# A fused retention and channel-mix kernel: the mu transfers go to SyncE's queue, more products of zeros ahead of the first transposes, and the pieces in a new written order

## The chip, the cores and the metric

The kernel runs on one core of one Trainium2 chip. The metric is the device time of one execution in microseconds (us). TensorE (PE) multiplies matrices, VectorE (DVE) and ScalarE (ACT) work on elements, GpSimd (POOL) and SyncE (SP) issue transfers here; ACT issues some transfers too.

## The reference, cut to what matters

```python
# attention: batch 4, 8 heads, 768 steps, head size 64
for t in range(S):
    state = gamma[None, :, None, None] * state + np.einsum('bhd,bhe->bhde', k[:, :, t], v[:, :, t])
    y[:, :, t] = scale * np.einsum('bhd,bhde->bhe', q[:, :, t], state)
x = y with the heads side by side                       # (4, 768, 512)

# channel mix: model size 512, inner size 1024
xk = mu_k * x + (1.0 - mu_k) * x_prev                   # x_prev: x one step earlier
xr = mu_r * x + (1.0 - mu_r) * x_prev
k = np.maximum(xk @ w_k, 0.0)
v = k * k @ w_v
r = 1.0 / (1.0 + np.exp(-(xr @ w_r)))
return r * v
```

## The kernel before, in words

**Tiling.** The sequence of each batch is cut into blocks of 256 steps: 4 x 3 = 12 blocks, numbered n = 0 to 11. For each block q and k are loaded, cast to f16 and transposed on PE (or, for q and k of blocks 9 to 11, by the transfer engines). Scores are formed within the block, masked on DVE and multiplied by the scaled v; a state of the earlier steps is carried from block to block. The result y is scaled into xT (`yout`, L570 and L577), the difference to the step before is formed (`differ`, L592), mixed with mu (`mixed`, L618), and goes through three products: keys with w_k (`keys`, L632 and L642), gate with w_r (`gate`, L672) and values with w_v (`values`, L684). ACT applies relu (L651), square (L659, L663) and sigmoid (L678), DVE multiplies gate and values (`result`, L690), and SP stores (`store`, L697).

**Order.** Nothing is scheduled automatically. The string `ORDER` (L28 to L79) lists all pieces. A loop at the end of the function reads it word by word and writes the instructions of each piece; each engine runs its own in that order and waits on semaphores for what it needs. A word is a code, the numbers of block and part, behind `~` the engine (v, a, p, s) and behind `@` the banks of the eight PSUM banks that it writes. So a change in the order of the words counts only as far as it changes the order on one engine or queue, and a change of bank changes which earlier reader a writer waits for.

**The codes in question.** `lq`, `lk`, `lv` load q, k, v (`load`, L239); for block 0 the first halves of q and k (heads 0 to 3, `0.0.2`) are loaded as f32 by SP into a staging place (`EARLY`, L245) and cast by ACT (`cq`, `ck`, L262); the second halves (`0.2.4`) come by POOL. `Tq` and `Tk` are transposes on PE (L303 to L314), `Eq` and `Ek` copy them from PSUM on ACT (L262). `S` are the scores (L372, L385, L393), `M` the mask on DVE (L417), `C` the new state (L458), `U` its addition, `gy` the powers of gamma (`gy.1~a` on ACT, L776). `Qa` and `Qb` are relu and square on ACT, `X` the mixing and `O` the result on DVE, `R`, `V` and `K` products on PE, `s` the sigmoid.

**Products of zeros.** `z.N` (`zeros`, L755) multiplies zeros into a bank that is free; nobody reads the result. N // 4 of them are f32 products (L758) and N % 4 are f16 products (L765), each with 512 columns.

**mu.** The word `mu` issues four transfers of 1 KB (`load_mu`, L739): two halves each of mu_k and mu_r into 8 rows of `mu8`. `mt` turns them on PE (L748), and `me` copies them on ACT (L751). The first written words are `gy.0 lq.0.0.2~s mu lk.0.0.2~s cq.0.0.2~a`. Ahead of the order, `constants` (L729) has ACT issue the transfers of two tables and run a small activation on a tile `warm`, and DVE clear some tiles.

Of the kernel before, what the change touches and what calls it, by code (L numbers as in the profile page):

```python
# [44 lines left out]
Tq.7@23 Eq.7~a V.1.1.0@1 V.1.1.1 G.4~a Qb.2.0 dx.3~v V.0.0.1 Tk.5@2 Ek.5~a D.4~v dx.4~v V.0.1.1
Qb.2.3 V.1.0.1 Tq.5@2 X.3.0.3 X.3.0.1 X.3.0.2 Eq.5~a X.3.0.0 K.3.1@3 Qa.3.1 K.3.3@4 O.1.1 O.0.0
S.5.0@01 O.1.0 O.0.1 lv.5~p lq.6~p M.5.0~v S.5.1@23 vs.5~v K.3.2@5 Qa.3.3 lk.6~p Qb.3.3 K.3.5@4
M.5.1~v X.2.1.0 Qa.3.2 X.2.1.2 Tq.6@67 Qa.3.5 Tk.6@01 Eq.6~a lv.6~p lv.7~p Ek.6~a C.5@5 U.5.0
X.3.1.0 Qb.3.1 K.3.0@4 Qa.3.0 lk.7~p K.3.7@6 S.6@23 Qb.3.2 M.6~v I.5@01 Y.5 vs.6~v V.2.1.0@7
R.2.1@2 lv.10~p Qb.2.2 Qa.3.7 K.3.4@6 st.0.0 vs.7~v Qb.3.7 s.2.1 st.0.1 V.2.1.1 Tk.7@45 Qb.3.5  # L50
Qa.3.4 X.3.1.3 X.3.1.1 Qb.3.0 C.6@23 st.1.0 J.5 Ek.7~a X.3.1.2 R.2.0@6 lv.8~p U.6.0~a D.5~v
U.6.1 U.6.2 U.6.3 V.2.0.0@4 s.2.0 K.3.6@6 dx.5~v Qa.3.6 lq.8~p lk.8~p st.1.1 R.4.1@5 I.6@01
O.2.1 st.2.1 X.5.0.1 s.4.1 G.6~a V.2.0.1 O.2.0 X.5.1.0 X.5.0.3 R.3.1@6 s.3.1 C.7@23 U.7.0 S.7@45
Y.6 M.7~v V.3.1.0@7 X.5.0.2 D.6~v R.4.0@6 lk.9~p Qb.3.4 vs.8~v V.3.0.0@4 R.3.0@5 X.5.1.2 s.4.0
Qb.3.6 V.4.1.0@6 V.3.0.1 V.3.1.1 X.5.1.3 V.4.1.1 U.7.1 U.7.2 X.5.1.1 I.7@01 U.7.3 Tk.8@23 O.3.1
s.3.0 O.3.0 R.5.1@7 Ek.8~a st.3.1 lv.9~p dx.6~v X.5.0.0 s.5.1 C.8@45 Tq.8@23 Y.7 K.5.0@7 O.4.1
# [6 lines left out]
Qb.6.6 V.5.1.1 K.6.2@4 Qa.6.2 X.8.0.1 Qb.6.2 K.6.5@3 tq.9~s Qa.6.5 R.6.1@4 s.6.1 tq.11~s st.5.0
K.6.0@6 O.5.1 U.9.2 U.9.3 G.9~v R.6.0@7 s.6.0 R.7.1@4 Qb.6.4 s.7.1 st.5.1 K.8.3@7 Qa.8.3 S.9@23
tk.11~s I.9@45 Qa.6.0 Qb.6.0 Qb.6.5 C.10@01 U.10.0 M.9~v R.7.0@7 s.7.0 U.10.1 U.10.2 U.10.3
K.8.2@6 K.8.1@2 Qa.8.1 vs.11~v Qb.8.1 V.6.0.0@7 Y.9 I.10@01 C.11@23 G.10~v V.6.0.1 Qa.8.2
V.7.1.0@6 D.9~v K.8.0@4 Qa.8.0 Qb.8.0 Qb.8.2 U.11.0 U.11.1 U.11.2 V.7.1.1 dx.9~v O.7.1 st.7.1
Qb.8.3 I.11@23 Y.10 D.10~v dx.10~v X.9.0.0 S.11@45 M.11~v X.9.0.2 V.7.0.0@6 V.7.0.1 V.6.1.0@0
V.6.1.1 V.8.0.0@1 V.8.0.1 X.9.0.1 V.8.1.0@4 V.8.1.1 st.4.0 X.9.0.3 K.9.0@5 O.7.0 K.9.4@6 X.9.1.1
Qa.9.0 Qa.9.4 Qb.9.4 X.9.1.0 O.6.0 st.6.0 Qb.9.0 X.9.1.3 X.8.1.2 Y.11 X.9.1.2 O.6.1 K.9.2@5  # L70
Qa.9.2 Qb.9.2 K.9.6@6 Qa.9.6 X.8.1.3 K.9.7@7 Qa.9.7 Qb.9.7 K.9.1@0 Qa.9.1 Qb.9.1 K.9.3@5 Qa.9.3
Qb.9.3 R.10.0@7 R.9.1@0 s.9.1 st.6.1 D.11~v R.9.0@5 s.9.0 st.7.0 X.8.1.1 K.9.5@6 V.10.1.0@5
Qa.9.5 Qb.9.5 Qb.9.6 V.10.0.0@6 X.8.1.0 dx.11~v R.8.1@0 s.8.1 V.9.1.0@2 R.8.0@0 X.11.0.2
X.11.1.3 X.11.0.0 X.11.0.3 X.11.0.1 K.11.1@3 s.8.0 K.11.3@0 Qa.11.3 O.8.0 st.8.0 s.10.0
# [8 lines left out]
def kernel(  # L83
# [328 lines left out]
    def masked(e, n, *part):  # L412
        src, dst = scored(n, *part)
        if part:
            seen.setdefault(n, []).append((part + (0, NJ))[:3])
# [1 line left out]
        nc.vector.tensor_tensor(  # L417
            out=dst, in0=dst if n in SPLITM else src,
            in1=mask[:, None, None, :].to_broadcast(list(dst.shape)), op=ALU.mult,
# [319 lines left out]
    def load_mu(e):  # L739
        for w, x in enumerate((moe_mu_k, moe_mu_r)):  # L740
            y = x.rearrange("(x r c) -> x r c", x=2, c=D)
            for hp in range(2):
                nc.scalar.dma_start(
                    out=mu8[w * NCO : (w + 1) * NCO, low(hp)], in_=y[:, 1:3] if hp else y[:, 0:4:3]
                )

# [108 lines left out]
```

## Time and profile before

| | us |
|---|---|
| median of 3 runs | 155.42 (155.16 to 155.71) |
| the profiled execution, whole | 155.54 |
| its span, first to last instruction | 153.7 |
| PE busy | 147.1 |
| DVE busy | 128.1 |
| ACT busy | 94.4 |
| POOL busy | 62.1 |

The profile is one execution. Times in it count from the first instruction of its span. A row of the timeline has the start, the length, the engine, the line of the kernel, the operation, what is written from what is read, the shape, how many instructions are merged into the row, and in brackets how long the engine had been idle and what ended that. The chain of waits goes back from the last instruction to whatever released each step. Matmuls are pipelined and their ends are modelled, so a filled PE is not always PE at its peak. A name such as SPq or ACTq is the queue of an engine from which transfers are issued; q0, q1 and q10 are the transfer queues that POOL, SP and ACT feed.

### The profile page before, as it was taken

To read this page: it belongs to the slowest core of one execution; us is meant where nothing else is said; L and a number is where in the kernel's file an instruction comes from. 1 tells how busy PE (TensorE), PEld (TensorE's weight loads), DVE (VectorE), ACT (ScalarE), POOL (GpSimd) and SP (SyncE) were. 2 spreads that over 40 slices of the span, in tenths; PEclk is the share of its full clock that TensorE was granted. 3 is DMA by queue.
4 is the path that set the end of the run, shared out by engine and by line. 5 is a ranking of instruction groups with operands and counts; after the bars stand their busy time and mean duration, and the time that the engine had idled before them with its cause. 6 is when DMAs were issued, how large, how long until landed. Compare 5 with 4: busy or idle time off the path is not lost.

```text
span 153.7 us, 4956 instructions
## 1 busy us (share of the span) xinstructions
PE 147.1 (96%) x2129; PEld 82.7 (54%) x2129; DVE 128.1 (83%) x204; ACT 94.4 (61%) x172; POOL 62.1 (40%) x77
## 2 busy tenths in 40 slices
...
GB/s 138 264 234 194 182 237 235 157 196 203 194 188 203 249 226 194 11 236 156 255 178 249 219 156 161 183 62 106 35 4 141 0 70 141 0 0 136 68 205 136
DMA packets 56525, 23.83 MB, mean 155 GB/s; under 512 B 48056, under 2 KB 52024, under 8 KB 56504
## 3 DMA queue, kind: packets, MB, share of 16 engines
...
q1 hardware_dynamic: 10848, 8.26, 21.9%
q10 hardware_dynamic: 456, 0.32, 0.8%
...
q14 instruction: 5, 0.04, 0.1%
...
## 4 chain that ended last, share of the span: by engine, by line
PE 70%; DVE 14%; DMA 6%; ACT 4%; issue 2%; ACTq 2%; DVEq 0%
PE ps L684 24%; PE ps L672 12%; PE ps L632 10%; PE ps L642 9%; DMA kT<-k 6%; DVE a L417 3%; DVE xk L618 3%; DVE dx L592 2%; DVE vs L277 2%; PE ps L504 2%; PE ps L765 2%; DVE xT L577 2%; PE ps L308 2%; PE ps L372 1%; PE ps L303 1%
## 5 line engine op out<-in xcount | busy, mean ns | idle before, releaser
L684 PE MATMUL ps<-wv,k2s 128*128 128x512 f16 x184 | 43.9, 380 | 0.2 <-ACT kr L651 0.2
L651 ACT ACTIVATE kr<-ps 128x512 f32<-128x512 f32 x48 | 27.8, 594 | 23.4 <-PE ps L632 14.9
L684 PEld LDWEIGHTS <-k2s 128*128 128x128 f16 x184 | 17.3, 98 | 19.1
L690 DVE SCALAR_TENSOR_TENSOR os<-ps,rs 128x512 f32<-128x512 f32 x23 | 15.1, 683 | 12.9 <-PE ps L684 6.5
L672 PE MATMUL ps<-wr,xr 128*128 128x512 f16 x96 | 24.0, 380 | 0.0
L642 PE MATMUL ps<-xk,wk 128*128 128x256 f16 x192 | 23.6, 273 | 0.1
L256 POOL DMA_DIRECT2D v<-in_v_dram x20 | 18.0, 917 | 13.8 <-DVE vs L277 10.9
L632 PE MATMUL ps<-xk,wk 128*128 128x512 f16 x96 | 22.8, 380 | 0.0
L417 DVE TENSOR_TENSOR a<-ps,c_sb 128x1024 f16<-128x1024 f32 (+1 forms) x20 | 21.8, 1109 | 0.8 <-PE ps L393 0.8
L678 ACT ACTIVATE rs<-ps 128x512 f32<-128x512 f32 x24 | 14.3, 594 | 11.4 <-PE ps L672 8.8
L642 PEld LDWEIGHTS <-wk 128*128 128x128 f16 x192 | 18.1, 98 | 4.4 <-DVE xk L618 0.5
L618 DVE SCALAR_TENSOR_TENSOR xr<-dx,mu,xT 128x256 f16<-128x256 f32 (+1 forms) x36 | 19.3, 564 | 0.0
L618 DVE SCALAR_TENSOR_TENSOR xk<-dx,mu,xT 128x256 f16<-128x256 f32 (+1 forms) x36 | 18.9, 567 | 0.3
L256 POOL DMA_DIRECT2D k<-in_k_dram x20 | 17.8, 916 | 2.6 <-DMA wv<-in_moe_w_v_dram 1.2
L277 DVE TENSOR_TENSOR vs<-v,csm_sb 128x1024 f16<-128x1024 f32 x12 | 14.5, 1214 | 2.7 <-DMA v<-in_v_dram 2.7
L659 ACT ACTIVATE k2s<-kr 128x512 f16<-128x512 f32 x24 | 14.7, 626 | 0.4
L592 DVE TENSOR_TENSOR dx<-xT 128x1024 f32<-128x1024 f32 x12 | 14.6, 1219 | 0.2
L663 ACT ACTIVATE k2s<-kr 128x512 f16<-128x512 f32 x24 | 14.5, 626 | 0.3
L632 PEld LDWEIGHTS <-wk 128*128 128x128 f16 x96 | 9.0, 98 | 10.5 <-issue 0.2
L672 PEld LDWEIGHTS <-xr 128*128 128x128 f16 x96 | 9.0, 98 | 10.0
L262 ACT COPY qT<-ps 128x1024 f16<-128x1024 f16 (+1 forms) x10 | 9.2, 925 | 7.5 <-PE ps L314 3.4
L262 ACT COPY kT<-ps 128x1024 f16<-128x1024 f16 (+1 forms) x10 | 9.3, 934 | 7.1 <-PE ps L303 3.4
...
## 6 DMA issues: line engine op xcount, KB each, us to landing
out_dram<-os SPq DMA_DIRECT2D x23, 256.0 KB, 3.9
v<-in_v_dram POOLq DMA_DIRECT2D x20, 256.0 KB, 6.3
k<-in_k_dram POOLq DMA_DIRECT2D x21, 128.0 KB, 7.1
q<-in_q_dram POOLq DMA_DIRECT2D x13, 128.0 KB, 7.4
q<-in_q_dram POOLq DMA_DIRECT2D x5, 256.0 KB, 8.1
...
wk<-in_moe_w_k_dram POOLq DMA_DIRECT2D x2, 256.0 KB, 9.6
```

Of the source, the lines that this page charges most:

```text
L256: e.dma_start(out=to[:, i, hs], in_=src[:, i])
L262: e.copy(out=out, in_=in_)
L277: e.tensor_tensor(out=VS(n), in0=V32(n).rearrange("p (h i d) -> p i h d", i=2, h=H), in1=gks[:, int(half(n) or wide(n)), :, :, None].to_br ...
L417: nc.vector.tensor_tensor(out=dst, in0=dst if n in SPLITM else src, in1=mask[:, None, None, :].to_broadcast(list(dst.shape)), op=ALU.mult,)
L592: e.tensor_tensor(out=DX(k)[:, :, m * TM + t0 : m * TM + t1], in0=x[:, :, c + t0 : c + t1], in1=x[:, :, c - 1 + t0 : c - 1 + t1], op=ALU.s ...
L618: nc.vector.scalar_tensor_tensor(out=XM[w](k)[:, j, t0:t1], in0=DX(k)[:, j, t0:t1], scalar=mu[:, w * NCO + j : w * NCO + j + 1], in1=x[:, ...
L632: nc.tensor.matmul(banks("K", n, g), lhsT=wk16[:, co, g * P : g * P + P], rhs=XM[0](k)[:, co, :], start=(co == 0), stop=(co == NCO - 1),)
L642: nc.tensor.matmul(pz[:, i, :], lhsT=wk16[:, co, fo * P : fo * P + P], rhs=XM[0](k)[:, co, m * TM + t0 : m * TM + t1], start=(i == 0 and c ...
L651: nc.scalar.activation(out=kr, in_=banks("K", n, g, *u), func=AF.Relu)
L672: nc.tensor.matmul(banks("R", n, tb), lhsT=XM[1](k)[:, co, t : t + P], rhs=wr16[:, co, :], start=(co == 0), stop=(co == NCO - 1),)
L684: nc.tensor.matmul(banks("V", n, tb), lhsT=K2(n)[:, fo, tb * P : tb * P + P], rhs=wv16[:, fo, :], start=(fo == 0), stop=(fo == NFO - 1),)
L690: nc.vector.scalar_tensor_tensor(out=OS(2 * n + tb), in0=banks("V", n, tb), scalar=1.0 / (KSC * KSC), in1=RS(2 * n + tb), op0=ALU.mult, op ...
```

## The change

The four mu transfers are issued by whatever engine the word names, and it now names SP. The word stands between the loads of q and k of block 0, which SP issues too, so the four come between them. `z.8` ahead of `Tq.0.0.2` becomes `z.9`, and `z.3` ahead of `Tk.0.0.2` becomes `z.5`. The third group, a `z.3` behind the k transposes, stays, and the fourth, another `z.3`, writes bank 1 instead of 4.

The words behind that stand in a new order. On each engine it differs from the old one in few places: PE runs `V.5.1.0` ahead of `V.5.0.0` with their banks exchanged; DVE runs `X.2.0.2` ahead of `X.2.0.0` and `O.6.0` two mixes earlier; ACT runs `Qb.2.0` ahead of `Eq.7` and `G.4`; POOL issues `lk.11` behind `lq.9` and `lq.11`. From block 6 on many banks are numbered differently. Where that changes the earlier user of a bank, it concerns `S.10`, `K.6.6`, `I.9`, `C.10`, `R.11.1`, `V.11.0.0` and `R.11.0`; the last of these now takes a bank that `O.9.0` reads. A helper for another kind of key product is added (`keys_by_row`, code `Kp`) and a list `KP`; the order names neither.

```diff
 ORDER = """
-gy.0 lq.0.0.2~s mu lk.0.0.2~s cq.0.0.2~a lv.0~p z.8@7 Tq.0.0.2@0 ck.0.0.2~a vs.0~v Eq.0.0.2~a
-z.3@1 Tk.0.0.2@1 Ek.0.0.2~a z.3@2 S.0.0.0.2@23 lk.0.2.4~p S.0.1.0.2@45 M.0.1.0.2~v Tk.0.2.4@1
+gy.0 lq.0.0.2~s cq.0.0.2~a mu~s lk.0.0.2~s ck.0.0.2~a lv.0~p z.9@7 Tq.0.0.2@0 Eq.0.0.2~a vs.0~v
+z.5@1 Tk.0.0.2@1 Ek.0.0.2~a z.3@2 S.0.0.0.2@23 lk.0.2.4~p S.0.1.0.2@45 M.0.1.0.2~v Tk.0.2.4@1
 gy.1~a Ek.0.2.4~a lq.0.2.4~p C.0@67 Tq.0.2.4@0 Eq.0.2.4~a U.0.0~v lv.1~p lk.1~p M.0.0.0.2~v
-U.0.1 z.3@4 S.0.1.2.4@45 M.0.1.2.4~v I.0@01 mt@2 me lq.1~p S.0.0.2.4@67 M.0.0.2.4~v lq.2~p G.0~a
+U.0.1 z.3@1 S.0.1.2.4@45 M.0.1.2.4~v I.0@01 mt@2 me S.0.0.2.4@67 lq.1~p M.0.0.2.4~v lq.2~p G.0~a
...
-U.8.2 R.5.0@7 tk.9~s s.5.0 X.6.0.0 V.4.0.0@6 V.4.0.1 O.4.0 Qb.5.1 lk.11~p lq.9~p Qb.5.3
-V.5.0.0@7 V.5.1.0@2 S.8@01 M.8~v I.8@45 X.6.1.3 Qb.5.2 V.5.0.1 K.6.4@6 X.6.1.1 O.5.0 Qa.6.4
...
+tk.10~s lv.11~p U.8.0 U.8.1 U.8.2 R.5.0@7 tk.9~s s.5.0 X.6.0.0 V.4.0.0@6 V.4.0.1 O.4.0 Qb.5.1
+V.5.1.0@7 lq.9~p Qb.5.3 V.5.0.0@2 S.8@01 M.8~v I.8@45 X.6.1.3 Qb.5.2 V.5.0.1 K.6.4@6 X.6.1.1
...
-R.11.1@0 V.11.0.0@7 R.11.0@4 O.9.0 st.9.0 V.11.0.1 O.10.1 s.11.1 st.10.1 s.11.0 O.10.0 st.10.0
+O.9.0 R.11.1@3 V.11.0.0@0 R.11.0@5 st.9.0 V.11.0.1 O.10.1 s.11.1 st.10.1 s.11.0 O.10.0 st.10.0
...
             for hp in range(2):
-                nc.scalar.dma_start(
+                (e or nc.scalar).dma_start(
                     out=mu8[w * NCO : (w + 1) * NCO, low(hp)], in_=y[:, 1:3] if hp else y[:, 0:4:3]
                 )
```

More of the change, by code (lines that the diff above doesn't have):

```diff
@@ L26 @@
 SPLITM = ()
+KP = ()
 DT = (9, 10, 11)
 ORDER = """
-gy.0 lq.0.0.2~s mu lk.0.0.2~s cq.0.0.2~a lv.0~p z.8@7 Tq.0.0.2@0 ck.0.0.2~a vs.0~v Eq.0.0.2~a
-z.3@1 Tk.0.0.2@1 Ek.0.0.2~a z.3@2 S.0.0.0.2@23 lk.0.2.4~p S.0.1.0.2@45 M.0.1.0.2~v Tk.0.2.4@1
+gy.0 lq.0.0.2~s cq.0.0.2~a mu~s lk.0.0.2~s ck.0.0.2~a lv.0~p z.9@7 Tq.0.0.2@0 Eq.0.0.2~a vs.0~v
+z.5@1 Tk.0.0.2@1 Ek.0.0.2~a z.3@2 S.0.0.0.2@23 lk.0.2.4~p S.0.1.0.2@45 M.0.1.0.2~v Tk.0.2.4@1
 gy.1~a Ek.0.2.4~a lq.0.2.4~p C.0@67 Tq.0.2.4@0 Eq.0.2.4~a U.0.0~v lv.1~p lk.1~p M.0.0.0.2~v
-U.0.1 z.3@4 S.0.1.2.4@45 M.0.1.2.4~v I.0@01 mt@2 me lq.1~p S.0.0.2.4@67 M.0.0.2.4~v lq.2~p G.0~a
+U.0.1 z.3@1 S.0.1.2.4@45 M.0.1.2.4~v I.0@01 mt@2 me S.0.0.2.4@67 lq.1~p M.0.0.2.4~v lq.2~p G.0~a
 vs.1~v z.4@3 Y.0 Tk.1@6 Ek.1~a D.0~v dx.0~v z.3@3 Tq.1@7 X.0.0.0 Eq.1~a X.0.1.1 wk.1~p C.1@23
-U.1.0 lk.2~p z.4@4 S.1.1@45 M.1.1~v z.1@0 I.1@01 wk.0~p S.1.0@67 M.1.0~v X.0.0.3 Tq.2@4 Eq.2~a
+U.1.0 lk.2~p z.4@4 S.1.1@45 wk.0~p M.1.1~v z.1@0 I.1@01 S.1.0@67 M.1.0~v X.0.0.3 Tq.2@4 Eq.2~a
 z.2@5 Y.1 lv.2~p X.0.0.1 X.0.0.2 z.1@5 K.0.2@4 Tk.2@5 D.1~v X.0.1.0 dx.1~v Qa.0.2 X.0.1.2
-X.1.0.0 Ek.2~a K.0.3@0 Qa.0.3 Qb.0.3 X.1.0.2 X.1.0.1 S.2.1@67 K.0.0@5 Qa.0.0 K.0.1@0 X.1.0.3
+X.1.0.0 K.0.3@0 Ek.2~a Qa.0.3 Qb.0.3 X.1.0.2 X.1.0.1 S.2.1@67 K.0.0@5 Qa.0.0 K.0.1@0 X.1.0.3
 K.1.2@1 K.1.0@5 Qb.0.0 wr~p X.1.1.0 Qa.0.1 U.1.1 G.1~a vs.2~v X.0.1.3 Qa.1.0 Qa.1.2 Qb.0.1
@@ L40 @@
 R.1.0@2 R.1.1@3 Qb.1.1 s.1.0 Tq.3@2 s.1.1 Eq.3~a C.3@67 Tk.3@4 Ek.3~a R.0.0@3 s.0.0 Tk.4@2
-S.3.0@01 wv.0~p dx.2~v X.2.0.0 X.2.0.2 X.2.0.1 X.2.0.3 X.2.1.1 S.3.1@45 Ek.4~a K.2.0@3 lq.7~p
+S.3.0@01 wv.0~p dx.2~v X.2.0.2 X.2.0.0 X.2.0.1 X.2.0.3 X.2.1.1 S.3.1@45 Ek.4~a K.2.0@3 lq.7~p
 Tq.4@2 M.3.1~v U.3.0~a U.3.1 Qa.2.0 wv.1~p Eq.4~a K.2.3@6 Qa.2.3 M.3.0~v K.2.1@7 S.4.1@45
 S.4.0@23 vs.4~v M.4.0~v K.2.2@6 Qb.0.2 I.3@01 Y.3 C.4@23 G.3~a M.4.1~v U.4.0 lk.5~p Qb.1.0
-Qa.2.2 V.1.0.0@6 lq.5~p I.4@45 Qa.2.1 Qb.2.1 X.2.1.3 J.3 D.3~v Y.4 V.0.1.0@7 V.0.0.0@0 J.4 U.4.1
@@ L45 @@
[L45 to L56, printed above, removed]
@@ L57 @@
-vs.9~v st.4.1 Eq.8~a D.7~v K.5.3@6 dx.7~v X.6.0.2 G.7~v Qa.5.0 Qb.5.0 st.2.0 lq.10~p tq.10~s
-K.5.1@7 Qa.5.1 X.6.0.3 X.6.0.1 Qa.5.3 K.5.2@2 Qa.5.2 st.3.0 lk.10~p tk.10~s lv.11~p U.8.0 U.8.1
-U.8.2 R.5.0@7 tk.9~s s.5.0 X.6.0.0 V.4.0.0@6 V.4.0.1 O.4.0 Qb.5.1 lk.11~p lq.9~p Qb.5.3
-V.5.0.0@7 V.5.1.0@2 S.8@01 M.8~v I.8@45 X.6.1.3 Qb.5.2 V.5.0.1 K.6.4@6 X.6.1.1 O.5.0 Qa.6.4
-K.6.7@3 Qa.6.7 K.6.3@6 Qa.6.3 X.6.1.0 lq.11~p X.6.1.2 K.6.1@3 Qa.6.1 Y.8 D.8~v C.9@01 Qb.6.1
-vs.10~v U.9.0~a S.10@67 M.10~v U.9.1 dx.8~v X.8.0.3 X.8.0.2 Qb.6.3 K.6.6@3 X.8.0.0 Qb.6.7 Qa.6.6
@@ L63 @@
[L63 to L74, printed above, removed]
@@ L75 @@
-V.9.0.0@1 Qa.11.1 Qb.11.1 K.11.2@0 Qa.11.2 O.8.1 st.8.1 K.11.0@7 X.11.1.2 V.10.0.1 Qb.11.2
-Qb.11.3 V.9.1.1 Qa.11.0 R.10.1@0 Qb.11.0 V.10.1.1 O.9.1 st.9.1 s.10.1 X.11.1.0 X.11.1.1 V.9.0.1
-R.11.1@0 V.11.0.0@7 R.11.0@4 O.9.0 st.9.0 V.11.0.1 O.10.1 s.11.1 st.10.1 s.11.0 O.10.0 st.10.0
-O.11.0 st.11.0 Vc.11.1.0@4 Oc.11.1.0 sc.11.1.0~s Vc.11.1.1@6 Oc.11.1.1 sc.11.1.1~a
+Qa.2.2 V.1.0.0@6 lq.5~p I.4@45 Qa.2.1 Qb.2.1 X.2.1.3 J.3 D.3~v Y.4 V.0.1.0@7 Qb.2.0 V.0.0.0@0
+J.4 U.4.1 Tq.7@23 Eq.7~a V.1.1.0@1 V.1.1.1 G.4~a dx.3~v V.0.0.1 Tk.5@2 Ek.5~a D.4~v dx.4~v
@@ new lines @@
+V.0.1.1 Qb.2.3 V.1.0.1 Tq.5@2 X.3.0.3 X.3.0.1 X.3.0.2 Eq.5~a X.3.0.0 K.3.1@3 Qa.3.1 K.3.3@4
+O.1.1 O.0.0 S.5.0@01 O.1.0 O.0.1 lv.5~p lq.6~p M.5.0~v S.5.1@23 vs.5~v K.3.2@5 Qa.3.3 lk.6~p
+Qb.3.3 K.3.5@4 M.5.1~v X.2.1.0 Qa.3.2 X.2.1.2 Tq.6@67 Qa.3.5 Tk.6@01 Eq.6~a lv.6~p lv.7~p Ek.6~a
+C.5@5 U.5.0 X.3.1.0 Qb.3.1 K.3.0@4 Qa.3.0 lk.7~p K.3.7@6 S.6@23 Qb.3.2 M.6~v I.5@01 Y.5 vs.6~v
+V.2.1.0@7 R.2.1@2 lv.10~p Qb.2.2 Qa.3.7 K.3.4@6 st.0.0 vs.7~v Qb.3.7 s.2.1 st.0.1 V.2.1.1
+Tk.7@45 Qb.3.5 Qa.3.4 X.3.1.3 X.3.1.1 Qb.3.0 C.6@23 st.1.0 J.5 Ek.7~a X.3.1.2 R.2.0@6 lv.8~p
@@ new lines @@
+U.6.0~a D.5~v U.6.1 U.6.2 U.6.3 V.2.0.0@4 s.2.0 K.3.6@6 dx.5~v Qa.3.6 lq.8~p lk.8~p st.1.1
+R.4.1@5 I.6@01 O.2.1 st.2.1 X.5.0.1 s.4.1 G.6~a V.2.0.1 O.2.0 X.5.1.0 X.5.0.3 R.3.1@6 s.3.1
+C.7@23 U.7.0 S.7@45 Y.6 M.7~v V.3.1.0@7 X.5.0.2 D.6~v R.4.0@6 V.3.0.0@4 lk.9~p Qb.3.4 vs.8~v
+R.3.0@5 X.5.1.2 s.4.0 Qb.3.6 V.4.1.0@6 V.3.0.1 V.3.1.1 X.5.1.3 V.4.1.1 U.7.1 U.7.2 X.5.1.1
+I.7@01 U.7.3 Tk.8@23 O.3.1 s.3.0 O.3.0 Ek.8~a R.5.1@7 st.3.1 lv.9~p dx.6~v X.5.0.0 s.5.1 C.8@45
+Tq.8@23 Y.7 K.5.0@7 O.4.1 vs.9~v st.4.1 Eq.8~a D.7~v K.5.3@6 dx.7~v X.6.0.2 G.7~v Qa.5.0 Qb.5.0
@@ new lines @@
+st.2.0 lq.10~p tq.10~s K.5.1@7 Qa.5.1 X.6.0.3 X.6.0.1 Qa.5.3 K.5.2@2 Qa.5.2 st.3.0 lk.10~p
+tk.10~s lv.11~p U.8.0 U.8.1 U.8.2 R.5.0@7 tk.9~s s.5.0 X.6.0.0 V.4.0.0@6 V.4.0.1 O.4.0 Qb.5.1
+V.5.1.0@7 lq.9~p Qb.5.3 V.5.0.0@2 S.8@01 M.8~v I.8@45 X.6.1.3 Qb.5.2 V.5.0.1 K.6.4@6 X.6.1.1
+O.5.0 Qa.6.4 K.6.7@3 Qa.6.7 K.6.3@6 Qa.6.3 X.6.1.0 lq.11~p X.6.1.2 K.6.1@3 Qa.6.1 Y.8 D.8~v
+C.9@01 Qb.6.1 vs.10~v U.9.0~a S.10@23 M.10~v U.9.1 dx.8~v X.8.0.3 X.8.0.2 Qb.6.3 K.6.6@6 X.8.0.0
+Qb.6.7 Qa.6.6 Qb.6.6 V.5.1.1 K.6.2@4 lk.11~p Qa.6.2 X.8.0.1 Qb.6.2 K.6.5@6 tq.9~s Qa.6.5 R.6.1@4
@@ new lines @@
+s.6.1 tq.11~s st.5.0 K.6.0@2 O.5.1 U.9.2 U.9.3 G.9~v R.6.0@3 s.6.0 R.7.1@4 Qb.6.4 s.7.1 st.5.1
+K.8.3@3 Qa.8.3 S.9@67 tk.11~s I.9@01 Qa.6.0 Qb.6.0 Qb.6.5 C.10@45 U.10.0 R.7.0@3 M.9~v s.7.0
+U.10.1 U.10.2 U.10.3 K.8.2@2 K.8.1@6 Qa.8.1 vs.11~v Qb.8.1 V.6.0.0@3 Y.9 I.10@45 C.11@67 G.10~v
+V.6.0.1 Qa.8.2 V.7.1.0@2 D.9~v K.8.0@0 Qa.8.0 Qb.8.0 Qb.8.2 U.11.0 U.11.1 U.11.2 V.7.1.1 dx.9~v
+O.7.1 st.7.1 Qb.8.3 I.11@67 Y.10 D.10~v dx.10~v X.9.0.0 S.11@01 M.11~v X.9.0.2 V.7.0.0@2 V.7.0.1
+V.6.1.0@4 V.6.1.1 V.8.0.0@5 V.8.0.1 X.9.0.1 V.8.1.0@0 V.8.1.1 st.4.0 X.9.0.3 K.9.0@1 O.7.0
@@ new lines @@
+K.9.4@2 O.6.0 st.6.0 X.9.1.1 Qa.9.0 Qa.9.4 Qb.9.4 X.9.1.0 Qb.9.0 X.9.1.3 X.8.1.2 Y.11 X.9.1.2
+O.6.1 K.9.2@1 Qa.9.2 Qb.9.2 K.9.6@2 Qa.9.6 X.8.1.3 K.9.7@3 Qa.9.7 Qb.9.7 K.9.1@4 Qa.9.1 Qb.9.1
+K.9.3@1 Qa.9.3 Qb.9.3 R.10.0@3 R.9.1@4 s.9.1 st.6.1 D.11~v R.9.0@1 s.9.0 st.7.0 X.8.1.1 K.9.5@2
+V.10.1.0@1 Qa.9.5 Qb.9.5 Qb.9.6 V.10.0.0@2 X.8.1.0 dx.11~v R.8.1@4 s.8.1 V.9.1.0@6 R.8.0@4
+X.11.0.2 X.11.1.3 X.11.0.0 X.11.0.3 X.11.0.1 K.11.1@7 s.8.0 K.11.3@4 Qa.11.3 O.8.0 st.8.0 s.10.0
+V.9.0.0@5 Qa.11.1 Qb.11.1 K.11.2@4 Qa.11.2 O.8.1 st.8.1 K.11.0@3 X.11.1.2 V.10.0.1 Qb.11.2
@@ L79 @@
+Qb.11.3 V.9.1.1 Qa.11.0 R.10.1@4 Qb.11.0 V.10.1.1 O.9.1 st.9.1 s.10.1 X.11.1.0 X.11.1.1 V.9.0.1
+O.9.0 R.11.1@3 V.11.0.0@0 R.11.0@5 st.9.0 V.11.0.1 O.10.1 s.11.1 st.10.1 s.11.0 O.10.0 st.10.0
+O.11.0 st.11.0 Vc.11.1.0@5 Oc.11.1.0 sc.11.1.0~s Vc.11.1.1@2 Oc.11.1.1 sc.11.1.1~a
 """
```

16 lines of the change are left out of this document (15 added, 1 removed).

## The prediction

> **What bounds the kernel now.** I read the page first, then a table of busy times by stretch, the chain of waits, the timeline of the first 13 us, and the landing times of single transfers.
>
> ```profile
> PE 147.1 (96%) x2129; PEld 82.7 (54%) x2129; DVE 128.1 (83%) x204; ACT 94.4 (61%) x172; POOL 62.1 (40%) x77
> PE 70%; DVE 14%; DMA 6%; ACT 4%; issue 2%; ACTq 2%; DVEq 0%
> ```
>
> TensorE (PE) is busy for 96% of the span, and 70% of the chain lies on it. That is an average. The busy times by stretch show who leads where (after the stretch and its length: PE, weight loads, DVE, ACT, POOL).
>
> ```profile
> 10.00:28.40 18.40, 17.44 (x352) 11.41 (x350) 18.09 (x29) 10.88 (x23) 12.96 (x17) 1.00 1.49 205
> 28.40:60.00 31.60, 31.44 (x455) 19.57 (x456) 30.95 (x42) 24.75 (x44) 20.21 (x24) 1.00 1.66 210
> 90.00:120.00 30.00, 29.54 (x544) 16.36 (x544) 27.57 (x42) 16.15 (x29) 0.00 (x0) 1.00 0.63 98
> ```
>
> From 10.0 to 28.4 VectorE (DVE) has 18.09 of 18.40 us filled; from 28.4 to 60 PE has 31.44 of 31.60, and from 90 to 120 it has 29.54 of 30.00. So these stretches have no room: what starts late there ends late. Only the first 10 us have gaps, and there the chain of waits (start, length, what) runs over ACT's queue:
>
> ```profile
> 3.63 0.62 ACTq L743
> 4.28 0.62 ACTq L743
> 4.94 0.63 ACT q L262
> 5.61 0.64 PE ps L314 x8
> ```
>
> The last two of the four mu transfers are being issued by ScalarE (ACT) until 4.90, and only then the cast of q starts. Both edits lie here:
>
> ```profile
> 0.74 0.45 SPq L245 DMA_DIRECT2D k2s<-in_q_dram  x1
> 1.05 3.78 PE L758 MATMUL ps<-zero 128*128 128x512 f32 x4 [1.05 <-DVE xT L737]
> 1.25 0.49 SPq L245 DMA_DIRECT2D k2s<-in_k_dram  x1
> 2.93 0.20 ACT L735 ACTIVATE warm<-warm 128x1 f32<-128x1 f32 x1
> 5.47 0.61 ACT L262 CAST k<-k2s 128x512 f16<-128x512 f32 x1
> 6.18 1.46 PE L765 MATMUL ps<-zero 128*128 128x512 f16 x3
> 7.57 0.64 PE L314 MATMUL ps<-c_sb,k 128*64 128x128 f16 x8
> 8.14 1.46 PE L765 MATMUL ps<-zero 128*128 128x512 f16 x3
> 8.26 0.59 ACT L262 COPY kT<-ps 128x512 f16<-128x512 f16 x1 [1.37 <-PE ps L314]
> 8.74 1.28 ACT L776 ACTIVATE gy_sb<-gy_sb,csm_sb 128x128 f32<-128x128 f32 x4
> 9.53 0.42 PE L393 MATMUL ps<-qT,kT 64*64 64x128 f16 x16
> 9.88 0.42 PE L314 MATMUL ps<-c_sb,k 128*64 128x128 f16 x8
> 10.34 0.58 ACT L262 COPY kT<-ps 128x512 f16<-128x512 f16 x1 [0.33 <-PE ps L314]
> 10.95 0.82 PE L765 MATMUL ps<-zero 128*128 128x512 f16 x3
> 11.06 0.58 ACT L262 COPY qT<-ps 128x512 f16<-128x512 f16 x1
> 11.70 0.31 PE L393 MATMUL ps<-qT,kT 64*64 64x128 f16 x8
> 12.06 1.29 DVE L417 TENSOR_TENSOR a<-ps,c_sb 128x512 f16<-128x512 f32 x2
> ```
>
> Read from this: k was cast at 5.47 to 6.08, but its transposes began at 7.57, when three products of zeros were over. So k has 1.5 us of slack against PE. From the kT copy at 8.26, ACT goes through the powers (8.74), the second kT (10.34) and the second qT (11.06); the scores of heads 4 to 7 follow at 11.70 and their mask on DVE at 12.06. From there DVE runs without a gap.
>
> **The change, part by part.** *The mu transfers.* ACT loses four issues. Its q cast can start when q has landed and the activation "warm" is over (2.93 + 0.20 = 3.13).
>
> ```profile
> k2s<-in_q_dram SPq DMA_DIRECT2D x1, 256.0 KB, 3.3
> k2s<-in_k_dram SPq DMA_DIRECT2D x1, 256.0 KB, 4.0
> c_sb<-c ACTq DMA_DIRECT2D x1, 144.0 KB, 3.3
> k<-in_k_dram POOLq DMA_DIRECT2D x1, 128.0 KB, 6.2
> ```
>
> These are times from issue to landing. q lands at 0.74 + 3.3 = 4.04, so the cast comes about 0.9 us earlier than 4.94 and ends near 4.7. The identity (c_sb, issued at 1.15) lands near 4.45.
>
> SyncE (SP) gains the same four issues, and they stand ahead of the k transfer. One mu issue takes 0.62, and they follow each other at 0.65 (3.63, 4.28). With that pitch the k transfer moves from 1.25 to 1.25 + 4 x 0.65 = 3.85. How long it then takes to land is not shown by any row, because POOL's transfers are under way by then. The lower end is q's 3.3 (landing 7.15), the upper end the 6.2 of a POOL transfer issued beside it at 2.28 (landing 10.05). What speaks for more than k's own 4.0 is that small transfers were slow in that stretch:
>
> ```profile
> q0 software_dynamic: 233, 0.32, 117.3%
> q10 hardware_dynamic: 6, 0.00, 0.6%
> ```
>
> This is the traffic from 8 to 9 us (queue, packets, MB, share of the 16 engines): POOL's queue (q0) fills the engines, and on ACT's queue (q10) six packets are still moving, although its last load, the fourth mu transfer of 1 KB, was issued at 4.28. I take the middle of the ends, 4.75: k lands at 3.85 + 4.75 = 8.60, where it landed at 1.25 + 4.0 = 5.25 before.
>
> The Trainium skill, "DMA: Bandwidth & Descriptors", section "Issuing engines are not separate DMA queues", says that another issuing engine saves only issue time, since all transfers share the same 16 engines. By that alone k would keep its 4.0 and land at 7.85, and the sum below would give +0.35 in place of +1.1.
>
> *What queues behind the late k.* ACT's order is: cast q, cast k, qT, kT, powers, second kT, second qT. The cast of k waits, and the copy of the finished q transposes waits behind it, though nothing needs qT before kT. SP's own next transfer is a store far behind. mu, issued earlier than before, is needed only behind the scores at 11.70. From a landing at 8.60, with starts as far apart as in the rows above: cast k 8.65 to 9.26; qT from 9.18 (0.53 behind, as 5.47 stood behind 4.94); k transposes on PE at 9.30; kT 0.46 later (10.34 stood 0.46 behind its transposes at 9.88) at 9.76; powers 0.48 later (8.74 after 8.26) at 10.24; second kT 1.2 later (the 1.28 of the powers less the 0.1 by which starts overlap) at 11.45, done at 12.03. The fourth group of zeros now writes the bank that this copy reads (bank 1 in place of 4), so PE starts it at 12.08, and its three products at about 0.23 each put the scores at 12.78. Before, these stood at 11.70: the mask on DVE moves from 12.06 to about 13.14, **+1.1 us**. In short, the shift is k's landing minus 7.5. Everything on DVE follows in order, and then PE at 28.40:
>
> ```profile
> 27.21 1.15 DVE vs L277
> 28.36 0.04 issue
> 28.40 0.32 PE ps L447 x8
> ```
>
> *The zeros.* z.8 becomes z.9: one more f16 product, 0.43 to 0.49 at the slow pace of 6.18 (three in 1.46). It fills the 0.78 us between 4.83 and 5.61 in which PE waited for q; the q transposes start near 5.3 and not at 5.61. Ahead of the k transposes z.3 becomes z.5: an f32 product (3.78/2 = 1.9) and an f16 one, 2.3 at the slow pace. From 5.3 + 0.57 it ends at 8.2 at the latest, ahead of 9.30: it costs nothing while k is late. If k came early, it would hold PE up to 0.6 longer than the 7.57 of before.
>
> *PE's pace.* Three f16 products took 1.46 at 8.14 and 0.82 at 10.95. The pace changed at about 9.5, after 3.9 us of work without a pause since 5.61. In the new order PE works without a pause from 1.05 to about 8, so I take the faster pace for the k transposes at 9.30. If it were still slow there, PE would be the limit: transposes 0.57 (as from 5.61 to 6.18), zeros 1.39 (8.14 to 9.53), then scores and second transposes at about twice the 0.35 from 9.53 to 9.88. The second kT would come at 9.30 + 0.57 + 1.39 + 1.4 = 12.66 in place of 11.45: 1.2 us on top.
>
> The Trainium skill, "TensorE: Matmul & The Clock Gate", section "What's actually happening", puts a busy window of about 3.4 us ahead of the full clock, free-running; an estimate from it is full clock by 7.9 (a window that starts by 4.5). The row of 9.5 agrees, and by it the sum stays at +1.1.
>
> *The rest of the written order.* On each engine it is almost the old one. PE swaps two halves of block 5 and takes other banks; DVE has one mix and one result earlier; ACT squares one tile ahead of a copy that waited anyway; POOL issues one k load behind two q loads.
>
> ```profile
> 48.24 1.01 ACT L262 COPY qT<-ps 128x1024 f16<-128x1024 f16 x1 [3.25 <-PE ps L303]
> 96.32 0.45 PE L372 MATMUL ps<-qT,kT 64*64 64x64 f16 x32 [0.35 <-DMA kT<-k]
> 145.36 1.89 DVE L690 SCALAR_TENSOR_TENSOR os<-ps,rs 128x512 f32<-128x512 f32 x3 [1.11 <-PE ps L684]
> 146.89 1.03 PE L672 MATMUL ps<-wr,xr 128*128 128x512 f16 x4
> ```
>
> The square goes into the 3.25 us of idle; uncovered it would be 0.63. The last gate product now takes the bank that the first of the three results at 145.36 (to about 146.0) reads, and starts at 146.89: 0.85 of cover. The one wait of PE that another load order could touch is the 0.35 at 96.32, for better or worse. I cost these together at 0, with ends of -0.35 and +0.35.
>
> **The sum.** The profiled execution took 155.54: 153.7 of span and 1.84 around it. It plus 1.1 is 156.6; it lies 0.12 above the median of the runs (155.42), so for the median I forecast 155.42 + 1.1 = **156.5**.
>
> **Rivals.**
> - *k lands far later* (6.2 as POOL's, or slow products on top): 10.05 - 7.5 = +2.55, about 158.0. For it: the mu packets above. Against it: k's packets are spread over all engines. 0.14.
> - *k is hardly hindered* (3.3 to 4.0 to land): -0.35 to +0.35, 155.1 to 155.8. For it: both SP rows of before. Against it: these transfers ran while POOL's queue was only starting. 0.18. The skill's rule on issuing engines points here, to the upper end of this case.
> - *Faster, because SP issues quickly.* Its small store at the end shows 0.33:
>
> ```profile
> 150.14 0.33 SPq L717 DMA_DIRECT2D out_dram<-os  x1
> ```
>
>  At 0.36 per issue k goes out at 2.69 and lands at 5.99. Then zeros decide: k transposes near 7.3 with the pace changing on the way, kT 7.76, powers 8.24, second kT 9.45, scores near 10.8, and DVE about 0.85 earlier: 154.6. It gains from a landing below 7.5. Against it: the 0.62 of mu itself, twice the store's. 0.14.
> - *The shift doesn't reach the end*, because a later wait for a transfer takes it up, such as that at 96.32 (0.35), or one that no row shows: 155.4 to 155.9. Against it: PE's full stretches. 0.08.
>
> The forecast itself (landing between 8.0 and 9.4) has 0.46: 155.9 to 157.3. The range 155.0 to 158.1 leaves out most of the faster case and the far end of the late one. About 0.3%, 0.47 us, is what can be told from no change: faster 0.15, same 0.23 (unhindered k and the lost shift, less their upper edges), slower 0.62.
>
> **What would show it.** Right: on SP four mu issues of about 0.62 and k's at 3.85; the casts on ACT near 4.1 and 8.6 with a long wait for the k transfer between; the first mask of heads 4 to 7 near 13.1; PE taking over from DVE near 29.5; nothing different behind that. Wrong: SP's issues at 0.4 or less, k landing below 7.5, f16 products of zeros at 0.4 and more each behind 9.5, or a shift at 28.4 that is gone at 120.

## The result, and the profile after

| | before | after |
|---|---|---|
| median | 155.37 us (155.16 to 155.71, 4 runs) | 161.28 us (160.97 to 162.05, 4 runs) |
| the profiled execution, whole | 155.54 us | 162.05 us |
| its span | 153.7 us | 160.3 us |

The ratio is 1.0386, with a 95% interval from 1.0342 to 1.043: slower by 3.9%, some 5.9 us. The ratios, here and below, leave out slow runs, more than 1.5% above the fastest of their kernel: one of the four of e1 (162.22 us) and three of the kernel before beside e9 and e10. The forecast of 156.5 had the sign, the place and the chain, but the time lies above the top of its range.

The page of after, with the rows of the engines (busy time, share of the span, instructions) and the shares of the chain:

```profile
PE 147.4 (92%) x2130; PEld 83.3 (52%) x2130; DVE 128.2 (80%) x204; ACT 94.4 (59%) x172; POOL 62.1 (39%) x77
PE 73%; DMA 11%; DVE 10%; SPq 2%; issue 1%; ACT 0%; DVEq 0%
```

No engine has more work: PE is busy 147.4 us (147.1 before) and DVE 128.2 (128.1), while the span grew by 6.6. Nearly all of it is waiting. On the chain, transfers rose from 6% to 11%, and SP's queue now appears, which did not before.

The timeline of after, its first 20 us, cut to the rows that answer to those of before:

```profile
1.26 1.47 SPq L757 DMA_DIRECT2D mu<-in_moe_mu_k_dram  x2
2.76 1.27 SPq L757 DMA_DIRECT2D mu<-in_moe_mu_r_dram  x2
3.98 0.62 ACT L263 CAST q<-k2s 128x512 f16<-128x512 f32 x1 [0.86 <-DMA k2s<-in_q_dram]
4.07 0.40 SPq L246 DMA_DIRECT2D k2s<-in_k_dram  x1
5.96 0.38 PE L779 MATMUL ps<-zero 128*128 128x512 f16 x1
11.42 0.62 ACT L263 CAST k<-k2s 128x512 f16<-128x512 f32 x1 [6.82 <-DMA k2s<-in_k_dram]
12.10 0.64 PE L315 MATMUL ps<-c_sb,k 128*64 128x128 f16 x8 [5.75 <-ACT k L263]
12.66 1.46 PE L779 MATMUL ps<-zero 128*128 128x512 f16 x3
15.30 0.58 ACT L263 COPY kT<-ps 128x512 f16<-128x512 f16 x1 [0.77 <-PE ps L315]
16.34 1.41 PE L779 MATMUL ps<-zero 128*128 128x512 f16 x3
18.04 1.29 DVE L418 TENSOR_TENSOR a<-ps,c_sb 128x512 f16<-128x512 f32 x2 [0.81 <-PE ps L394]
```

Read it from the top. SP issues the four mu transfers from 1.26 on and k at 4.07. ACT casts q at 3.98, almost a microsecond earlier than before. Then ACT waits 6.82 us for k. PE ends its last product of zeros at 5.96 + 0.38 = 6.34 and stands still for 5.75 us, behind the cast of k. When it goes on at 12.10, three f16 products of zeros take 1.46 and the next three 1.41: PE is at its slow pace. The mask of heads 4 to 7 on DVE comes at 18.04, where it came at 12.06 before: +5.98.

The chain of waits of after (start, length, what), at four places:

```profile
4.07 7.33 DMA k2s<-in_k_dram
...
33.20 1.14 DVE vs L278
34.39 0.32 PE ps L448 x8
...
92.54 10.80 DMA kT<-k
103.39 0.45 PE ps L373 x32
...
156.99 0.42 DVE os L723
```

The transfer of k takes 7.33 us from issue to landing. PE takes over from DVE at 34.39 (28.40 before), so +5.99: nothing between 18 and 34 us makes up for it. The scores of block 10 come at 103.39 (96.32 before), +7.07; here PE waits 1.76 us for a turned kT, 0.35 before. The last result starts at 156.99; the corresponding row of before reads

```profile
150.56 0.42 DVE os L709
```

and the difference is +6.43. So +5.98 at the first mask is nearly the whole of it.

The granted clock in stretches of 4 us of after (the number ahead of the last two; PE's busy time is the first after the length):

```profile
8.00:12.00 4.00, 0.00 (x0) 0.00 (x0) 0.49 (x1) 0.58 (x2) 2.63 (x5) 0.84 1.46 245
12.00:16.00 4.00, 3.90 (x73) 2.22 (x75) 0.82 (x2) 2.87 (x8) 2.12 (x4) 0.50 1.57 193
16.00:20.00 4.00, 4.00 (x69) 1.80 (x66) 3.19 (x6) 1.71 (x6) 3.15 (x5) 0.80 1.75 185
```

From 8 to 12 PE does nothing. Taken in steps of half a microsecond the same column reads 1.00 up to 10.5, 0.74 from 10.5 to 11.0 and 0.50 from there to 17.5, then 0.94 from 17.5 to 18.0 and 1.00 behind it. So the clock was halved at about 10.7 and came back at about 17.6, which gives the 0.84, 0.50 and 0.80 above. Between 12.10 and 17.6 PE works through the critical transposes at half pace.

The loss therefore has two parts. By the prediction's own count the mask shifts by k's landing minus 7.5: that is 11.40 - 7.5 = +3.9 for the landing. The other 2.1 of the 5.98 are left for the pace, which e6 tests.

### The profile page after: what moved, and what is told of

Its sections match the earlier page's. It is cut to its first block, busy times and chain, and to the rows that moved or that the text cites. A ratio compares the mean times of both kernels' runs of the same rounds, so it can differ in the third digit from the quotient of the medians.

```text
span 160.3 us, 4956 instructions
## 1 busy us (share of the span) xinstructions
PE 147.4 (92%) x2130; PEld 83.3 (52%) x2130; DVE 128.2 (80%) x204; ACT 94.4 (59%) x172; POOL 62.1 (39%) x77
## 4 chain that ended last, share of the span: by engine, by line
PE 73%; DMA 11%; DVE 10%; SPq 2%; issue 1%; ACT 0%; DVEq 0%
PE ps L698 23%; PE ps L686 13%; PE ps L633 11%; PE ps L643 10%; DMA kT<-k 7%; DMA k2s<-in_k_dram 5%; PE ps L505 2%; DVE a L418 2%; DVE xk L619 2%; PE ps L309 2%; PE ps L779 2%; SPq L757 2%; DVE xT L578 2%; DVE dx L593 1%; PE ps L542 1%; DVE vs L278 1%
## 5 line engine op out<-in xcount | busy, mean ns | idle before, releaser
L633 PEld LDWEIGHTS <-wk 128*128 128x128 f16 x96 | 9.0, 98 | 10.5 <-issue 0.2
(73 smaller groups left out, 154.8 us busy)
```

The lines of the kernel that those rows point to most:

```text
L633: nc.tensor.matmul(banks("K", n, g), lhsT=wk16[:, co, g * P : g * P + P], rhs=XM[0](k)[:, co, :], start=(co == 0), stop=(co == NCO - 1),)
```

## The experiments

Two theories on the late k: **A**, POOL's transfers, which are under way by then, hold it up; **B**, the four small transfers ahead of it in SP's own queue do. A third point is the pace: that its loss costs about 2 us on top. Each ratio is against the kernel before, run beside it on the same chip; its medians were 155.36, 155.36 and 154.8 us in the three groups (e1 to e4, e5 to e8, e9 and e10).

**e1: the mu transfers alone.** The kernel before, with only the four issues moved ahead of k's; zeros and order are the old ones.

```diff
-gy.0 lq.0.0.2~s mu lk.0.0.2~s
+gy.0 lq.0.0.2~s mu~s lk.0.0.2~s
-                nc.scalar.dma_start(
+                (e or nc.scalar).dma_start(
```

> The old order with one edit: the word mu names SP and stands between the loads of q and k, zeros and everything else as before. Theory (the late k does all of it): the k transfer is issued near 4.1, lands near 11, and the time is 160.5 to 162. Rival (the new order of the pieces or the zeros cost several us): 155.2 to 156.5.

Measured: 159.76 to 161.37 us in three runs, ratio 1.0341 (1.0258 to 1.0425). k's issue and its landing, from the profile of the run of 162.22 us:

```profile
4.07 0.41 SPq L245 DMA_DIRECT2D k2s<-in_k_dram  x1
```

```profile
k2s<-in_k_dram SPq DMA_DIRECT2D x1, 256.0 KB, 8.2
```

So the move of mu by itself makes the loss; the more zeros and the new order aren't needed for it.

**e2: the changed kernel with mu behind k.**

```diff
-mu~s lk.0.0.2~s ck.0.0.2~a
+lk.0.0.2~s mu~s ck.0.0.2~a
```

> The new kernel with the four mu transfers behind the k transfer on SP, all else as changed. Theory (k's lateness is all): k is issued at 1.26 and lands near 5.2, its cast starts at 5.3 or earlier, and the time is 154.6 to 155.6. Rival (SP as the issuer of mu, or the new order, costs by itself): above 157.

Measured: 154.66 us (153.88 to 154.98), ratio 0.9953 (0.9915 to 0.999). k is issued at 1.26 and lands 4.0 later; the mask stands at 11.28:

```profile
1.26 0.49 SPq L246 DMA_DIRECT2D k2s<-in_k_dram  x1
11.28 1.29 DVE L418 TENSOR_TENSOR a<-ps,c_sb 128x512 f16<-128x512 f32 x2 [0.17 <-PE ps L394]
```

Exchanging two words of the order takes 6.6 us away from the changed kernel, and what remains is a little faster than before.

**e3: the changed kernel with mu on ACT again.**

```diff
-cq.0.0.2~a mu~s lk.0.0.2~s ck.0.0.2~a
+mu lk.0.0.2~s cq.0.0.2~a ck.0.0.2~a
```

> The new kernel with mu back on ACT ahead of the cast of q, k second on SP; the zeros and the written order as changed. Theory: 155.2 to 156.0, since k lands near 5.2 as before; the zeros cost at most 0.6 us. Rival (the order costs): above 157.

Measured: 154.31 us (153.97 to 155.35), ratio 0.9966 (0.9929 to 1.0004): not told apart from before, far from slower, and below the 155.2 that was expected at least. Here only the zeros and the written order are left of the change. Together they cost nothing.

**e4: k late, with nothing ahead of it.** The kernel before, where a write of one element per partition to k's staging place, put among DVE's powers, holds k's issue until about 4 us. SP's queue has nothing between q and k.

```diff
+            if l == 2:
+                nc.vector.memset(staged(1)[:, 0, 0:1], 0.0)
```

> The old kernel with mu on ACT, and one tiny DVE write into k's staging place that lets SP issue the k transfer only near 4 us, with nothing ahead of it on SP but q. Theory A (POOL's packets fill the engines from 3.5 us): k takes about 7 us to land, at 11, and the time is near 160. Theory B (k's packets stand behind the slow mu transfers in SP's own queue): k lands 4.0 to 4.8 after its issue, at 8.0 to 8.8, and the time is 156 to 158.

Measured: 160.19 us (159.68 and 160.69), ratio 1.0311 (1.0214 to 1.0408). The issue in the timeline of e4, k's landing in its list of transfers (last number: from issue to landing) and the traffic from 4.4 to 7.0 us (queue, packets, MB, share of the 16 engines):

```profile
3.96 0.38 SPq L245 DMA_DIRECT2D k2s<-in_k_dram  x1
```

```profile
k2s<-in_k_dram SPq DMA_DIRECT2D x1, 256.0 KB, 7.4
```

```profile
q0 software_dynamic: 729, 0.58, 116.2%
q10 hardware_dynamic: 9, 0.00, 0.4%
```

Issued at 3.96 with an empty queue ahead, k takes as long as behind mu (7.4 against 7.33). In the 2.6 us behind its issue there is no row for SP's queue (q1) at all: not one of k's packets moves while POOL's queue (q0) moves 729. B falls here, and A stands.

**e5: the changed kernel with POOL's transfers held.** A write to the place of v, put behind the powers on DVE, holds POOL's first load until 5.61. SP's queue is that of the changed kernel, mu ahead of k.

```diff
+            if l == 6:
+                nc.vector.memset(V32(0)[:, 0:1], 0.0)
```

> The new kernel with one tiny DVE write into POOL's first destination behind the powers, so that POOL's loads begin near 5.1 and not at 1.26. Theory A (k waits for POOL's traffic): k, still issued near 4.1 behind the four mu transfers, lands in 3.3 to 4.5, near 7.5 to 8.5. Theory B (k stands behind mu in SP's queue): it still takes about 7. The time itself says little, as all of POOL's loads come later: 157 to 161.

The timeline of e5, k's landing and the traffic from 4.2 to 7.0:

```profile
4.10 0.40 SPq L246 DMA_DIRECT2D k2s<-in_k_dram  x1
5.61 1.03 POOL L252 DMA_DIRECT2D v<-in_v_dram  x1 [5.17 <-DVE v L802]
6.92 0.62 ACT L263 CAST k<-k2s 128x512 f16<-128x512 f32 x1 [2.33 <-DMA k2s<-in_k_dram]
```

```profile
k2s<-in_k_dram SPq DMA_DIRECT2D x1, 256.0 KB, 2.8
```

```profile
q1 hardware_dynamic: 539, 0.26, 31.7%
```

k, issued at 4.10 behind the same four transfers, lands in 2.8 us, sooner than the 3.3 that was expected at least: now only SP's queue has a row, and k's packets begin at about 5.2, 1.1 us behind the issue. In the changed kernel the same stretch of traffic reads

```profile
q0 software_dynamic: 870, 0.65, 120.0%
q1 hardware_dynamic: 12, 0.00, 0.5%
```

where the 12 packets, far below a hundredth of a MB, are not k, whose 0.26 MB come later. This is A from the other side. Its one time, 157.17 us, is not that of an early k: POOL's own loads come 4.3 us later here, and the first mask of heads 4 to 7 stands at 14.20, behind k's second half.

**e6: PE kept at work.** The changed kernel with 27 instead of 5 units of zeros ahead of the k transposes, six f32 and three f16 products, so that PE works nearly until k has come.

```diff
-z.5@1 Tk.0.0.2@1
+z.27@1 Tk.0.0.2@1
```

> The new kernel with 27 in place of 5 passes of zeros ahead of the k transposes, so that PE works through most of its 5.8 us wait for k. Theory (the pause costs PE its pace, and that 2.0 of the 6 us): products of zeros behind the k transposes at 0.27 each and not 0.46, the mask of heads 4 to 7 at 16.0 to 16.4 in place of 18.04, and 159.2 to 159.9 in all. Rival (the pace is hidden behind ACT's queue): no change, 160.9 to 162.

Measured: 160.05 us (159.34 and 160.76), ratio 1.0319 (1.0231 to 1.0407). The timeline of e6:

```profile
12.11 0.62 ACT L263 CAST k<-k2s 128x512 f16<-128x512 f32 x1 [7.54 <-DMA k2s<-in_k_dram]
12.79 0.41 PE L315 MATMUL ps<-c_sb,k 128*64 128x128 f16 x8 [0.44 <-ACT k L263]
13.13 0.82 PE L779 MATMUL ps<-zero 128*128 128x512 f16 x3
16.61 1.29 DVE L418 TENSOR_TENSOR a<-ps,c_sb 128x512 f16<-128x512 f32 x2 [0.17 <-PE ps L394]
```

The cast of k happens to come 0.7 us later than in the changed kernel, and the mask comes 1.4 us earlier. Three zeros take 0.82 and not 1.46. From k's landing (with which its cast starts) to the mask it takes 16.61 - 12.11 = 4.50 us, in the changed kernel 18.04 - 11.40 = 6.64. The difference, 2.1 us, is the price of the lost pace, and the 4.50 is what the prediction's sum had for this piece (13.14 - 8.60 = 4.54). The whole time gains less than 2.1 because k itself lands later (8.0 us from its issue here), which also put the mask 0.2 behind the 16.4 that was expected at most. Why k lands later was not tried; e1, with the old zeros, had 8.2.

**e7: two mu transfers ahead of k, two behind.** `load_mu` takes the number of the vector as an argument.

```diff
-cq.0.0.2~a mu~s lk.0.0.2~s ck.0.0.2~a
+cq.0.0.2~a mu.0~s lk.0.0.2~s mu.1~s ck.0.0.2~a
```

> The new kernel with two mu transfers ahead of k on SP and two behind, so that k goes out near 2.8. Theory A (k must be out before POOL's first packets at 3.5 to 4): its first packets come at about 3.5 to 4 beside POOL's first ones, and it lands between 5.5 and 9. If each 0.65 us of issue simply moved the landing by 0.65 it would be 6.7.

The timeline of e7:

```profile
2.79 0.40 SPq L246 DMA_DIRECT2D k2s<-in_k_dram  x1
9.58 0.62 ACT L263 CAST k<-k2s 128x512 f16<-128x512 f32 x1 [5.06 <-DMA k2s<-in_k_dram]
16.36 1.29 DVE L418 TENSOR_TENSOR a<-ps,c_sb 128x512 f16<-128x512 f32 x2 [0.98 <-PE ps L394]
```

One run: 160.09 us. k is issued 1.3 us earlier than in the changed kernel and lands 1.8 us earlier, at 9.56 and so behind the 5.5 to 9 that was expected, yet it still takes 6.8 us, where it takes 4.0 when issued at 1.25. So the step is not at mu's fourth transfer: 1.5 us of delay is enough to lose the place ahead of POOL. The pace is lost as well (16.36 - 9.58 = 6.8), although PE's pause is only 3.08 us here:

```profile
10.25 0.64 PE L315 MATMUL ps<-c_sb,k 128*64 128x128 f16 x8 [3.08 <-ACT k L263]
```

**e8: e2 with the old three zeros ahead of the k transposes.**

```diff
-mu~s lk.0.0.2~s ck.0.0.2~a
+lk.0.0.2~s mu~s ck.0.0.2~a
...
-z.5@1 Tk.0.0.2@1
+z.3@1 Tk.0.0.2@1
```

> The new kernel with mu behind k on SP and z.3 in place of z.5 ahead of the k transposes: a try to beat both kernels. k lands near 5.2; the k transposes start near 6.5 to 7.0 and not 7.45, the mask of heads 4 to 7 at 10.8 to 11.3, since the second half of k lands only near 8.5: 154.0 to 154.7. Rival (fewer zeros let PE fall back): 155.0 to 156.

Measured: 154.17 us (153.79 to 154.6, 12 runs), ratio 0.9952 (0.9921 to 0.9982). The timeline of e8:

```profile
7.16 0.41 PE L315 MATMUL ps<-c_sb,k 128*64 128x128 f16 x8
10.99 1.29 DVE L418 TENSOR_TENSOR a<-ps,c_sb 128x512 f16<-128x512 f32 x2
```

With k early, PE's zeros set the k transposes: they start at 7.16, where five units let them start at 7.45 (e2), and the mask stands at 10.99, 1.07 earlier than before. This version beats both kernels, by 0.2% to 0.8% against before.

**e9: v ahead on POOL's queue.** Is it only POOL's loads that convert to f16, in small packets, that hold k up (A1), or whatever POOL has in flight (A2)? e4 again, with the second v load, which converts nothing, moved ahead of POOL's two loads of block 0's second halves.

```diff
+            if l == 2:
+                nc.vector.memset(staged(1)[:, 0, 0:1], 0.0)
-S.0.0.0.2@23 lk.0.2.4~p
+S.0.0.0.2@23 lv.1~p lk.0.2.4~p
-U.0.0~v lv.1~p lk.1~p
+U.0.0~v lk.1~p
```

> The kernel of e4_k_late_alone (k issued near 4, nothing ahead of it on SP) with POOL's queue reordered: v of block 1 goes out ahead of the two halves of k and q of block 0 that POOL converts to f16 on the way. Theory A1 (k must wait until those many small converted packets are through, as in e4, where its first packets came at 7.0): they come later now, so k's first packets flow at 5 to 6 beside v's and it lands at 7 to 9. Theory A2 (any POOL packets ahead hold it): first packets at 7 or later and a landing at 10 to 12 again.

The traffic of e9 from 4.2 to 7.8 us:

```profile
q0 software_dynamic: 484, 1.02, 103.4%
q10 hardware_dynamic: 12, 0.00, 0.4%
```

k was issued at 3.98 and landed 6.9 us later, at about 10.9; one run took 159.39 us. POOL's packets in this stretch are large (1.02 MB in 484, some 2 KB each; in the changed kernel 0.65 MB in 870), and k moves none of its own all the same. A1 falls; A2 is nearer, though it doesn't say how the engines choose.

**e10: mu behind k, and nothing else.** The kernel before with mu on SP's queue behind k.

```diff
-gy.0 lq.0.0.2~s mu lk.0.0.2~s cq.0.0.2~a
+gy.0 lq.0.0.2~s lk.0.0.2~s mu~s cq.0.0.2~a
```

> The old kernel with one edit: the four mu transfers on SP, but behind k; zeros and order as before. If the gain of e2 and e8 comes from freeing ACT (q cast at 4.0 and not 4.9, k transposes near 6.9 and not 7.57): 154.3 to 154.9, mask of heads 4 to 7 near 11.4. If it comes from the zeros, which keep PE at work between 4.8 and 5.6: the same as before, 155.2 to 155.6.

Measured: 154.09 us (153.59 to 155.47, 12 runs), ratio 0.9974 (0.9943 to 1.0006). q is cast at 4.07 and the mask stands at 11.36, 0.7 earlier than before. The intervals of e2, e3, e8 and e10 overlap, so how the small gain divides between mu's move, the zeros and the order is open. e8's interval ends 0.2% below 1 and e2's 0.1% below it; those of e3 and e10 reach 1.

The runs side by side, by k's issue:

| kernel | k issued | ahead of it | issue to landing | mask minus landing |
|---|---|---|---|---|
| before | 1.25 | q | 4.0 | limited by PE |
| e7 | 2.79 | two of mu, POOL's loads | 6.8 | 6.8 |
| e4 | 3.96 | POOL's loads | 7.4 | 6.2 |
| e9 | 3.98 | POOL's loads, v first | 6.9 | 5.7 |
| after | 4.07 | four of mu, POOL's loads | 7.3 | 6.6 |
| e1 | 4.07 | four of mu, POOL's loads | 8.2 | 6.8 |
| e6 | 4.10 | four of mu, POOL's loads | 8.0 | 4.5 |
| e5 | 4.10 | four of mu | 2.8 | waits for POOL |

## Why the prediction was wrong

**Right: SP's issues.** A pitch of 0.65 put k's issue at 3.85; it came at 4.07, since the first mu issue ran longer (1.47 for the first two). The faster rival, with issues at 0.36, is out. Right too was the cast of q near 4.04 (3.98), with a long wait for k behind it.

**Wrong, the step that failed: the upper end of k's landing, and with it the middle.** The prediction bounded k's transfer time by q's 3.3 below and by the 6.2 of a POOL transfer above, and took the middle, 4.75. Measured were 7.33 in the changed kernel and 6.8 to 8.2 in every run where POOL's transfers were under way, all above the end that was to bound them. The 6.2 was the quickest of POOL's early loads, of 128 KB and issued at 2.28; POOL's k load of block 1, with k's 256 KB and issued at 4.64, close to where k was to go, took 7.5 in the profile of before already:

```profile
k<-in_k_dram POOLq DMA_DIRECT2D x1, 256.0 KB, 7.5
```

That row would have put k's landing at 11.35, where it came at 11.40, but that it fits so closely is luck: a row of POOL's own transfer bounds POOL's share of the engines, not that of a queue that has to get in beside it. Cost: 11.40 instead of 8.60, 2.8 us, of which the later issue has 0.2. By the Trainium skill, "DMA: Bandwidth & Descriptors", section "Issuing engines are not separate DMA queues", k would have kept its 4.0 (landing at 7.85); the measurement decides against reading it so: with the same issuing engine, the same bytes and the same four transfers ahead, k took 2.8 us in e5 and 7.33 in the changed kernel, and what differs is the traffic of another issuer.

**Wrong: the pace.** "In the new order PE works without a pause from 1.05 to about 8, so I take the faster pace for the k transposes at 9.30." The zeros were over at 6.34, since the pace had risen early (an f16 product at 5.96 took 0.38), and the late k made a pause of 5.75 us. This second step did not hang on the first alone: with k at 8.60 the pause would have been 9.30 - 6.34 = 3.0 us, and in e7 a pause of 3.08 was enough to lose the pace. The working had a price for it, 1.2 us on top; e6 shows 2.1, because not only the transposes and one group of zeros ran slowly, but all up to 17.6, the fourth group too. The Trainium skill, "TensorE: Matmul & The Clock Gate", section "What's actually happening", gives half clock after an idle window of about 3.4 us and full clock after a busy one. The trace of the changed kernel agrees with both: half at about 10.7, inside a pause that began at 6.34, and full again at 17.6, 5.5 us after work resumed at 12.10; the two lie 6.9 us apart, about two such windows. For the fall e7 and e9 do not agree: their granted clock was halved at about 9.3 and 8.0, only 2.2 and 1.2 us behind PE's last product (over at 7.17 and 6.80), so a whole idle window was not needed there, and the measurement decides. I had used that rule for the rise and not for the fall.

**Right: the count behind the landing.** 4.54 from landing to mask was measured as 4.50 where the pace was kept (e6).

**Right: no room behind.** DVE's full stretch carried +5.98 to PE's takeover as +5.99, and the end has +6.43. The 1.76 us wait for kT at 103.39 adds 1.1 and the last 50 us give 0.6 back; which of these belongs to the change was not tried, but the wait itself isn't special to it: it is 1.0 in e10, which has the old order, 1.0 in e2 and 1.4 in e3.

**Right: the rest of the written order at 0.** e3 holds all of it, with the zeros, and its interval reaches from 0.9929 to 1.0004; the loss that was allowed for, 0.35 us or 0.2%, lies outside. That the order alone is at 0 is not shown: e3's mask stands at 11.09, 0.97 us earlier than before, and a small loss behind it could hide in that gain.

**The rivals.** "k lands far later" was the right one of them, with its two causes. It was priced at 158.0, by 6.2 or by the slow products. Both came at once, and the first was larger. That the shift is taken up later did not happen. A landing hardly hindered is what k has when POOL is quiet (2.8, e5); what was held against that rival, that SP's loads of before ran while POOL's queue was only starting, is what decided.

**Still open.** How the packets of one queue come to wait while another's fill the engines. The runs show that k's first packets come 2.5 us and more behind its issue when POOL's transfers are under way (none up to 7.0 in the changed kernel and e4, none up to 7.8 in e9), not by what rule. Nor is it only the start: against e5 k takes 4.5 us longer, of which the later first packets (7.0 and not 5.2) are 1.8 and the slower rest 2.7. k on ACT's queue was not tried.
